# In the first of four batches, v of two heads as one stationary side; wide products of a pair's shared tile; the weights' clamp and rounding on other engines

## The chip, the cores and the metric

The kernel runs on one core of a Trainium2 chip, in one launch. The metric is device time in microseconds (us). Engines are named as in the profile: PE (TensorE matmul), PEld (its weight loads), DVE (VectorE), ACT (ScalarE), POOL (GpSimd), SP (the queue that issues most DMAs). All run side by side and wait for each other by semaphores; each takes its own instructions in program order.

## The reference

Three stages follow each other; everything is float32.

```
attention: B=4, H=8, S=576, D=64, blocks of 64, causal by block
  scores = q k^T / 8, masked where block(query) < block(key)
  attn = softmax(scores) (sum + 1e-9);  out = attn v;  x = out as (2304, 512)
first layer:  h = max(x w1, x w2, x w3);  x = h w_out        (512 -> 768 -> 512)
second layer: p = probs / sum(probs);  out = sum_e p_e * (relu(x w1_e) w2_e)   (4 experts, 512 -> 1024 -> 512)
```

## The kernel before

**Two halves for a float32 number.** A fast product type (F32R) keeps fewer bits than float32. Where precision matters, a number is split into a rounded high part and a low rest, and a product becomes three (high·high, high·low, low·high). The first batch of the attention works with plain float32 products instead, which PE carries out as two passes each: each such product shows as two MATMUL records, each with its own LDWEIGHTS.

**Attention.** Heads go in pairs (`NPAIR` is 4 pairs a batch, 16 in all). For a head, `scores` makes the transposed-sign score tiles (L250), takes row minima (DVE, L264), exponentials with row sums (ACT, L271), and leaves a `normalise` step (POOL, L282) for later. The last 64 queries of the two heads of a pair share one tile, `p4` (rows 0 to 63 are the even head's queries, 64 to 127 the odd one's). `turn_probs` transposes the probabilities on PE (L314) and evacuates them from PSUM into `eh` (batches 2 to 4: `eh` by ACT, L319, and the rest `el` by DVE, L320). Its part 2 is the shared tile: keys `j` = 0 to 4 by 128 columns, of which 64 belong to each head.

**The products with v.** `values` is the step that the change rewrites. In the first batch (`values32`, L341 and L345) the stationary side is one head's v block, 128 keys by 64 columns, so PE stands in a 128*64 arrangement; the fifth key block has 64 keys and gives 64*64. A head makes a 128-column product, then 384, 384, 128 and 256 columns, then five of 64 columns for its last 64 queries. All other products of the attention use 128 stationary columns. In batches 2 to 4 (L366, L374) the stationary side is `vs`, 128 columns: 64 of v's high part, 64 of its low part. `eh` and `el` are multiplied one after the other, and the last 64 queries take 5 products of 64 columns with `eh` and 5 with `el`. ACT copies half of the result (L385) and DVE adds the two halves (L386) into `xf`.

**The first layer.** `moe1(b)` runs as a filler between the steps of the next batch's attention, so many units per step (`UNITS`); in the last batch it runs by itself. Its products are L510, its running maximum L548 (DVE).

**The weights of the first layer** are computed once, in `Convert`: 26 pieces (18 of 512 columns for w1, w2, w3, 8 of 384 for w_out), beside the attention of batches 1 and 2. The inputs are 64-bit numbers, taken apart as words: per piece ACT makes `a` (L433) and `r` (L435); DVE clamps (L440), shifts (L442) and joins the sign (L443); POOL adds `r` (L447) and rounds to the high part (L82); DVE makes the low part (L457); a DMA stores both to `held`, from where batches 2 to 4 take them.

**What sets the order.** The code is recorded and a scheduler with a timeline of its own puts each engine's instructions in order, so an edit can move instructions that it does not touch. Buffers count too: the slots of `wt` (5), `r` (1), `a` (2) and `ps_x` (4 banks of PSUM) are reused when their last reader is done.

Of the kernel before, what the change touches and what calls it, by code (L numbers as in the profile page):

```python
# [25 lines left out]
def program(tc, q, k, v, w1, w2, w3, w_out, probs, e_w1, e_w2, out):  # L26
# [57 lines left out]
    def load_pair(g):  # L84
        b, h0 = divmod(2 * g, H)

        w = 2 * R * D
        o = (B - 1) * KD * S + g % 2 * w
        raw = arena[:, o:o + w].rearrange("p (r d) -> p r d", d=D)
        for n, src in ((0, q), (1, k)):  # L90
            for h, pp in ((0, lo), (1, hi)):
                nc.sync.dma_start(
                    out=raw[pp, n * R:(n + 1) * R],
                    in_=src[b, h0 + h].rearrange("(r p) d -> p r d", r=R),
                )
        vraw = ap_.tile([P, 2, 5, D], F32, name="vraw", tag="vraw", bufs=4)
        for h in range(2):
            nc.sync.dma_start(
                out=vraw[:, h, 0:4],
                in_=v[b, h0 + h, 0:512].rearrange("(j p) d -> p j d", p=P),  # L100
            )
        nc.sync.dma_start(
            out=vraw[hi, :, 4], in_=v[b, h0:h0 + 2, 512:S].rearrange("h p d -> p h d")
        )
        pairs[g] = dict(raw=raw, vraw=vraw)
# [19 lines left out]
    def prep_pair(g):  # L125
# [38 lines left out]
        for pp, js in ((both, slice(0, 4)), (hi, slice(4, 5))):  # L164
            vh = vs[pp, :, js, 0:64]
            rounded(nc.gpsimd, vh, vraw[pp, :, js])
            nc.gpsimd.tensor_tensor(vs[pp, :, js, 64:128], vraw[pp, :, js], f(vh), op=ALU.subtract)
# [131 lines left out]
    def turn_probs(g, part):  # L299
# [3 lines left out]
        w = (1024, 256, 640)[part]  # L303
        eh = ap_.tile([P, w], F32 if g < H else F32R, name="eh", tag=f"eh{part}", bufs=1)
        el = None if g < H else ap_.tile([P, w], F32R, name="el", tag=f"el{part}", bufs=1)
        (pairs[g // 2] if part == 2 else hd)["e", part] = (eh, el)
        pt = hd["p"] + [pairs[g // 2]["p4"]]
        for n in banks:
            o = 512 * (n - banks[0])
            tt = ps_x.tile([P, 512], F32, name="tt", tag="x")  # L310
            c = 0
            for j, i in BANKS[n]:
                k0 = S - P if j == 4 else j * P
                nc.tensor.transpose(tt[:, c:c + P], pt[i][:, k0:k0 + P], ident)  # L314
                c += P
            if g < H:
                (nc.scalar.copy if n else nc.vector.tensor_copy)(eh[:, o:o + c], tt[:, 0:c])
# [6 lines left out]
    def products(g, part):  # L324

        h = g % 2
        todo = []
        for j in KEYS[part]:
            q0 = max(P, P * j)
            todo.append((j, slice(q0 - P, 384), part, slice(BASE[j] + q0 - 512 * 2 * part, BASE[j] + 512 - 512 * 2 * part)))  # L330
        if part:
            todo += [(j, slice(384, 448), 2, slice(j * P + h * 64, j * P + h * 64 + 64)) for j in range(5)]
        return todo

    def values32(g, part):

        hd, vraw, h = heads[g], pairs[g // 2]["vraw"], g % 2
        if part == 0:
            hd["pv"] = [ps_v.tile([P, 512], F32, name=f"pv{i}", tag="v") for i in range(2)]
            et = hd["e", 0][0]  # L340
            nc.tensor.matmul(out=hd["pv"][0][lo, 0:P], lhsT=vraw[:, h, 0], rhs=et[:, 0:P], start=True, stop=True)  # L341
        for n, (j, to, which, of) in enumerate(products(g, part)):
            et = (pairs[g // 2] if which == 2 else hd)["e", which][0]
            rows = hi if j == 4 else both
            nc.tensor.matmul(  # L345
                out=hd["pv"][1][lo, to], lhsT=vraw[rows, h, j], rhs=et[rows, of],
                start=part == 0 and n == 0, stop=j == 4,
            )
# [3 lines left out]
        qs = (slice(0, P), slice(P, S))[part]  # L352
        nc.scalar.copy(xf[lo if h == 0 else hi, qs], hd["pv"][part][lo, 0:qs.stop - qs.start])
        if part:
            del heads[g]

    def values(g, part):
# [12 lines left out]
        todo = products(g, part)  # L370
        for n in range(2):
            for m, (j, to, which, of) in enumerate(todo):
                et = (pairs[g // 2] if which == 2 else hd)["e", which][n]
                nc.tensor.matmul(  # L374
                    out=pv[:, to], lhsT=vs[:, h, j], rhs=et[:, of],
                    start=part == 0 and n == 0 and m == 0, stop=part == 1 and n == 1 and j == 4,
                )
# [5 lines left out]
        src = hd["pv"][part][:, 0:qs.stop - qs.start]  # L383
        tmp = ap_.tile([P, S - P], F32, name="tmp", tag="tmp", bufs=1)[own, 0:qs.stop - qs.start]
        nc.scalar.copy(tmp, src[other])  # L385
        nc.vector.tensor_tensor(xf[own, qs], src[own], tmp, op=ALU.add)  # L386
        if part == 0:
            return
        del heads[g]
# [14 lines left out]
    class Convert:  # L404
# [32 lines left out]
        def second(self, i):  # L437
            a = self.buf(i, "a")
            au, high = a.bitcast(U32), self.words(i)[1]
            nc.vector.tensor_scalar(a, a, MOST, LEAST, op0=ALU.min, op1=ALU.max)  # L440
# [8 lines left out]
        def third(self, i):  # L449
# [6 lines left out]
            rounded(nc.gpsimd, high, a)  # L456
# [486 lines left out]
```

## Time and profile before

| | |
|---|---|
| median of 3 runs | 1324.93 us (1322.38 to 1325.15) |
| the profiled execution's time | 1325.09 us |
| its span | 1323.4 us |
| granted TensorE clock, mean | 0.991 |
| PE busy | 1286.8 us, 97% |
| PEld, DVE, POOL, ACT busy | 1185.8, 917.8, 629.9, 541.2 us |
| first to last product with v: batch 1 | 22.4 to 98.9 us |
| first to last product with v: batches 2 to 4 | 105.8 to 473.1 us |

A row of a group reads: line, engine, operation, tiles, shapes and count, then the busy time and the mean of one, then the idle time of the engine just before them and what ended it. A shape 128*64 is rows by columns of the stationary side; the one after it is partitions by moving columns. In a time line a row starts at the first number; how long a run of matmuls holds PE is read from its start to the start of the next row, because the ends overlap. Rows of waits give the total, the number and the longest.

### The profile page before, as it was taken

The page shows a single profiled execution, that of the slowest core. Times are in us where ns is not written, and L with a number is a line of the kernel's source. Part 1 is how long each engine was busy: PE and PEld are TensorE (multiplying, and loading weights), DVE is VectorE, ACT ScalarE, POOL GpSimd, SP SyncE. Part 2 cuts the span into 40 slices and gives each one's busy share as a digit, 9 for nine tenths or more (in the row PEclk, how much of TensorE's full clock was granted, in tenths as well). Part 3 has the DMA queues.
Part 4 walks back from the last instruction along what each step waited for, and adds up shares of the span by engine and source line. Part 5 has one row for each costly group of instructions (what it writes and reads, how often), then busy time and mean ns, then how long its engine had stood idle before and what let it go on. Part 6 is the DMA issues. An engine that isn't in the chain of part 4 may idle for free.

```text
span 1323.4 us, 20932 instructions
## 1 busy us (share of the span) xinstructions
PE 1286.8 (97%) x7670; PEld 1185.8 (90%) x7670; DVE 917.8 (69%) x1685; ACT 541.2 (41%) x1219; POOL 629.9 (48%) x639
## 2 busy tenths in 40 slices
PE   7899999999999999999999999999999999999998
PEld 5669889999999989988999998999999899999997
DVE  6878999555656562178767788777777876777753
ACT  5676666444544430143333343333333433333331
POOL 4965776333334342165444455444444644454420
PEclk9899999999999999999999999999999999999999
DMA  8746677555444355232222223222222133222211
GB/s 204 216 122 167 200 224 204 162 156 133 141 123 116 112 176 161 79 96 64 76 69 64 64 64 95 81 64 64 74 79 72 55 110 91 64 64 64 64 33 48
DMA packets 146982, 142.85 MB, mean 108 GB/s; under 512 B 64576, under 2 KB 112704, under 8 KB 146880
## 3 DMA queue, kind: packets, MB, share of 16 engines
q1 hardware_dynamic: 144480, 132.18, 34.0%
q10 hardware_dynamic: 2400, 9.34, 3.1%
q8 instruction: 60, 0.98, 0.3%
q14 instruction: 42, 0.34, 0.1%
HBM read 114.86 MB, written 17.30 MB: 100 GB/s over the span
## 4 chain that ended last, share of the span: by engine, by line
PE 79%; DVE 8%; issue 3%; DMA 3%; POOL 3%; ACT 2%; SPq 0%; ACTq 0%; POOLq 0%; DVEq 0%
PE m L796 24%; PE m L510 17%; PE o L861 10%; PE o L859 10%; PE o L860 10%; PE st L250 3%; PE pv L374 2%; PE tt L314 2%; DMA q<-q 1%; PE pv L345 1%; POOL p L282 1%; ACT p L271 1%; DVE arena L443 1%; DVE t L718 1%; DMA pr<-in_moe_domain_probs 1%
## 5 line engine op out<-in xcount | busy, mean ns | idle before, releaser
L510 PE MATMUL m<-xh,wt 128*128 128x288 f32 x1152 | 258.0, 302 | 6.5 <-DVE mt L548 5.5
L859 PE MATMUL o<-w2h,hh 128*128 128x512 f32 x576 | 225.4, 392 | 4.9 <-DVE arena L866 4.9
L861 PE MATMUL o<-w2h,hl 128*128 128x512 f32 x576 | 225.5, 392 | 1.3 <-DVE hl L824 1.3
L860 PE MATMUL o<-w2l,hh 128*128 128x512 f32 x576 | 225.2, 391 | 0.0
L510 PEld LDWEIGHTS m<-xh,wt 128*128 128x128 f32 x1152 | 191.4, 188 | 9.1 <-DVE mt L548 5.3
L824 DVE SCALAR_TENSOR_TENSOR hl<-c,hh 128x384 fp32r<-128x384 f32 x144 | 168.3, 1189 | 37.4 <-ACT hh L823 37.1
L689 POOL TENSOR_TENSOR w2l<-r,w2h 128x512 fp32r<-128x512 f32 x96 | 130.1, 1375 | 89.8 <-ACT w2h L688 89.8
L510 PE MATMUL m<-xl,wt 128*128 128x288 f32 x576 | 170.2, 295 | 0.0
L689 POOL TENSOR_TENSOR sl<-s,sh 128x1024 fp32r<-128x1024 f32 x48 | 116.6, 2429 | 77.5 <-ACT sh L688 77.5
L689 POOL TENSOR_TENSOR al<-r,ah 128x512 fp32r<-128x512 f32 x48 | 64.7, 1348 | 180.6 <-ACT ah L688 177.2
L866 DVE SCALAR_TENSOR_TENSOR arena<-o,pr,arena 128x512 f32<-128x512 f32 x126 | 93.6, 743 | 71.5 <-PE o L861 71.4
L859 PEld LDWEIGHTS o<-w2h,hh 128*128 128x128 f32 x576 | 108.6, 189 | 24.0 <-DVE arena L866 6.0
L861 PEld LDWEIGHTS o<-w2h,hl 128*128 128x128 f32 x576 | 108.5, 188 | 22.5 <-DVE hl L824 1.7
L823 ACT ACTIVATE hh<-c 128x384 fp32r<-128x384 f32 x144 | 71.0, 519 | 135.9 <-DVE c L818 135.9
L860 PEld LDWEIGHTS o<-w2l,hh 128*128 128x128 f32 x576 | 108.6, 189 | 17.8
L282 POOL TENSOR_SCALAR p<-p,sm 128x128 f32<-128x128 f32 (+2 forms) x144 | 89.4, 640 | 58.7 <-DVE sm L280 27.9
L510 PEld LDWEIGHTS m<-xl,wt 128*128 128x128 f32 x576 | 108.4, 188 | 0.7
L271 ACT ACTIVATE p<-st,mn 128x128 f32<-128x128 f32 (+3 forms) x144 | 78.7, 553 | 51.1 <-DVE mn L264 50.9
L688 ACT CAST ah<-r 128x512 fp32r<-128x512 f32 x48 | 29.8, 620 | 156.3 <-issue 124.2
L548 DVE TENSOR_TENSOR mt<-m,mt 128x288 f32<-128x288 f32 x96 | 43.5, 454 | 63.8 <-PE m L510 61.5
L510 PE MATMUL m<-hh,wo 128*128 128x288 f32 x384 | 84.5, 301 | 0.4 <-ACT arena L559 0.4
L688 ACT CAST w2h<-r 128x512 fp32r<-128x512 f32 x96 | 59.1, 619 | 44.3 <-PE o L861 35.0
(166 smaller groups left out, 3000.1 us busy)
## 6 DMA issues: line engine op xcount, KB each, us to landing
wt<-held SPq DMA_DIRECT2D x54, 512.0 KB, 4.0
r<-in_moe_w SPq DMA_DIRECT2D x48, 512.0 KB, 3.9
r<-in_moe_w SPq DMA_DIRECT2D x96, 256.0 KB, 2.7
arena<-in_moe_w SPq DMA_DIRECT2D x18, 512.0 KB, 4.5
held<-wt SPq DMA_DIRECT2D x18, 512.0 KB, 3.4
wo<-held SPq DMA_DIRECT2D x12, 768.0 KB, 4.3
q<-q ACTq DMA_DIRECT2D x26, 304.0 KB, 4.5
arena<-in_q SPq DMA_DIRECT2D x32, 144.0 KB, 3.3
```

What stands on the lines that cost most here:

```text
L271: nc.scalar.activation(x, st[:, o:o + w], ACTF.Exp, bias=mn[:, col:col + 1], scale=-1.0, accum_out=sm[:, col:col + 1],)
L282: nc.gpsimd.tensor_scalar(x, x, sm[:, col:col + 1], 1.0, op0=ALU.mult, op1=ALU.mult)
L510: nc.tensor.matmul(out=out_, lhsT=w, rhs=x, start=m == 0, stop=m == n - 1)
L688: nc.scalar.copy(dst_h, raw)
L689: (low or nc.gpsimd).tensor_tensor(dst_l, raw, f(dst_h), op=ALU.subtract)
L796: ins = nc.tensor.matmul(out=m, lhsT=w, rhs=x, start=start and n == 0, stop=stop and n == 3 * KH - 1, skip_group_check=True,)
L823: nc.scalar.activation(h, src, ACTF.Relu)
L824: nc.vector.scalar_tensor_tensor(l, src, 0.0, f(h), op0=ALU.max, op1=ALU.subtract)
L859: nc.tensor.matmul(out=o, lhsT=hh[:, ts], rhs=wh, start=i == 0, stop=False)
L860: nc.tensor.matmul(out=o, lhsT=hh[:, ts], rhs=wl, start=False, stop=False)
L861: nc.tensor.matmul(out=o, lhsT=hl[:, ts], rhs=wh, start=False, stop=i == G - 1)
L866: nc.vector.scalar_tensor_tensor(acc, ov, pr[:, tt, e:e + 1], acc, op0=ALU.mult, op1=ALU.add)
```

## The change

**First batch.** `vraw` is laid out key block by key block with the two heads side by side, so a stationary side is [128 keys, 128 columns] for both heads, and 64 result rows that belong to the other head are not used. Rows 0 to 63 of the fifth block are zeroed by POOL, and its product takes all 128 rows. The last 64 queries are left out of the even head and made once for the pair: five products of 128 columns (64 queries of each head) in the odd head. A head's rows are copied from where they lie, the odd head's with two more copies.

**Batches 2 to 4.** The shared tile is `e4`, with high and low part side by side. The five products of a head take 128 columns, high and low at once, instead of two times five of 64. The two results lie in columns 384 to 511: DVE adds the first half as before, and the second into `last`; in the odd head POOL adds `last` to `xf` for the pair.

**Weights.** The clamp goes from DVE to POOL, the rounding from POOL to ACT.

```diff
-        vraw = ap_.tile([P, 2, 5, D], F32, name="vraw", tag="vraw", bufs=4)
+        vraw = ap_.tile([P, 5, 2, D], F32, name="vraw", tag="vraw", bufs=4)
+        if g < NPAIR:
+            nc.gpsimd.memset(vraw[lo, 4], 0.0)
...
+        if part == 2:
+            e4 = ap_.tile([P, 5, 2, 2, 64], F32R, name="e4", tag="e4", bufs=1)
+            pairs[g // 2]["e4"] = e4
...
+            if part == 2:
+                j0, j1 = BANKS[n][0][0], BANKS[n][-1][0] + 1
+                high, low = (e4[:, j0:j1, :, x] for x in range(2))
+                src = tt[:, 0:c].rearrange("x (j h q) -> x j h q", h=2, q=64)
+                if g < H:
+                    nc.scalar.copy(f(high), src)
+                    continue
+                nc.scalar.copy(high, src)
+                nc.vector.tensor_tensor(low, src, f(high), op=ALU.subtract)
...
     def values32(g, part):
+        own = lo if h == 0 else hi
+        both_v = [vraw[:, j].rearrange("p h d -> p (h d)") for j in range(5)]
...
+        todo = [(j, to, et[:, of]) for j, to, of in products(part)]
+        if part and h:
+            todo += [(j, slice(384, 512), f(pairs[g // 2]["e4"][:, j, :, 0])) for j in range(5)]
+        for n, (j, to, x) in enumerate(todo):
             nc.tensor.matmul(
-                out=hd["pv"][1][lo, to], lhsT=vraw[rows, h, j], rhs=et[rows, of],
-                start=part == 0 and n == 0, stop=j == 4,
+                out=hd["pv"][1][:, to], lhsT=both_v[j], rhs=x,
+                start=part == 0 and n == 0, stop=part == 1 and n == len(todo) - 1,
             )
...
+        if h == 0:
+            nc.scalar.copy(xf[lo, P:512], pv[lo, 0:384])
+        else:
+            nc.scalar.copy(xf[hi, P:512], pv[hi, 0:384])
+            nc.scalar.copy(xf[lo, 512:S], pv[lo, 384:448])
+            nc.scalar.copy(xf[hi, 512:S], pv[hi, 448:512])
...
     def values(g, part):
+        todo = [(j, to, et[:, of]) for et in hd["e", part] for j, to, of in products(part)]
+        if part:
+            todo += [(j, slice(384, 512), pairs[g // 2]["e4"][:, j, h]) for j in range(5)]
+        for n, (j, to, x) in enumerate(todo):
+            nc.tensor.matmul(out=pv[:, to], lhsT=vs[:, h, j], rhs=x, start=part == 0 and n == 0, stop=j == 4)
...
+        last = pairs[g // 2]["last"]
+        nc.vector.tensor_tensor(last[own], src[own, w:n], tmp[:, w:n], op=ALU.add)
+        if h:
+            nc.gpsimd.tensor_tensor(xf[:, S - 64:S], xf[:, S - 64:S], last, op=ALU.add)
...
-            nc.vector.tensor_scalar(a, a, MOST, LEAST, op0=ALU.min, op1=ALU.max)
+            nc.gpsimd.tensor_scalar(a, a, MOST, LEAST, op0=ALU.min, op1=ALU.max)
...
-            rounded(nc.gpsimd, high, a)
+            rounded(nc.scalar, high, a)
```

The lines of the changed kernel are shifted: L341 and L345 become L359 and L368, L366 and L374 become L396 and L404, L385 and L386 become L414 and L415, L314 becomes L323, L176 L180, L250 L254; the clamp is L476 and the rounding L80.

**What stands in the queues.** PE, first batch, the end of an even head (`pv` is the result in PSUM, `tq` the transposes that prepare the next pair). Before:

```order
L345 MATMUL pv_612<-eh,vraw 64x256
L250 MATMUL st<-kk,q_376 128x256
L250 MATMUL st<-kk,q_377 128x256
L176 MATMUL tq<-idents,spare 128x128 x4
L345 MATMUL pv_612<-eh,vraw 64x64 x4
L176 MATMUL tq<-idents,spare 128x128 x8
L345 MATMUL pv_612<-eh,vraw 64x64
L176 MATMUL tq<-idents,spare 128x128 x6
```

Now:

```order
L368 MATMUL pv_613<-eh,vraw 128x256
L254 MATMUL st<-kk,q_380 128x256
L254 MATMUL st<-kk,q_381 128x256
L180 MATMUL tq<-idents,spare 128x128 x18
L323 MATMUL tt<-ident,p_489 128x128
```

The five narrow products are gone from the even head, and no row of 64 partitions is left between rows of 128. In the program before, the first batch's products with v stand in 32 such groups between other work.

PE, batch 2, its first head (`vs` is the split v). Before:

```order
L374 MATMUL pv_1206<-el,vs 128x128
L374 MATMUL pv_1206<-eh,vs 128x256
L374 MATMUL pv_1206<-eh,vs 128x64 x4
L250 MATMUL st<-kk,q_1096 128x128
L374 MATMUL pv_1206<-eh,vs 128x64
L374 MATMUL pv_1206<-el,vs 128x256
L374 MATMUL pv_1206<-el,vs 128x64 x5
```

Now:

```order
L404 MATMUL pv_1197<-el,vs 128x128
L404 MATMUL pv_1197<-eh,vs 128x256
L404 MATMUL pv_1197<-el,vs 128x256
L404 MATMUL pv_1197<-e_1184,vs 128x128 x4
L254 MATMUL st<-kk,q_1086 128x128
L404 MATMUL pv_1197<-e_1184,vs 128x128
```

Ten products of 64 columns became five of 128.

ACT, batch 2, the end of its second head (`arena` holds the conversion's `a` and `r`, `eh` the evacuated probabilities, `tmp` the copied half of a result). Before:

```order
L385 COPY tmp<-pv_1487 64x448
L319 CAST eh<-tt 128x512 x2
L319 CAST eh<-tt 128x256
L435 ACTIVATE arena<-arena 128x512
L319 CAST eh<-tt 128x512
L319 CAST eh<-tt 128x128
L385 COPY tmp<-pv_1659 64x128
```

Now:

```order
L414 COPY tmp<-pv_1475 64x512
L338 CAST eh<-tt 128x512 x2
L471 ACTIVATE arena<-arena 128x512
L80 CAST wt<-arena 128x512
L338 CAST eh<-tt 128x256
L469 ACTIVATE arena<-arena 128x512
L332 CAST e_1599<-tt 128x8x64
L332 CAST e_1599<-tt 128x2x64
L414 COPY tmp<-pv_1643 64x128
```

The rounding (L80) stands right behind `r` of the next piece (L471), ahead of evacuations. The last 4,387 products on PE, those from about 475 us of the span on, stand in the same order as before.

More of the change, by code (lines that the diff above doesn't have):

```diff
@@ L102, in load_pair @@
         nc.sync.dma_start(
-            out=vraw[hi, :, 4], in_=v[b, h0:h0 + 2, 512:S].rearrange("h p d -> p h d")
+            out=vraw[hi, 4], in_=v[b, h0:h0 + 2, 512:S].rearrange("h p d -> p h d")
         )
@@ L302, in turn_probs @@
         banks = PARTS[part]
[L303 to L306, printed above, removed]
+        if part == 2:
+            e4 = ap_.tile([P, 5, 2, 2, 64], F32R, name="e4", tag="e4", bufs=1)
+            pairs[g // 2]["e4"] = e4
+        else:
+            w = (1024, 256)[part]
+            eh = ap_.tile([P, w], F32 if g < H else F32R, name="eh", tag=f"eh{part}", bufs=1)
+            el = None if g < H else ap_.tile([P, w], F32R, name="el", tag=f"el{part}", bufs=1)
+            hd["e", part] = (eh, el)
         pt = hd["p"] + [pairs[g // 2]["p4"]]
@@ L322, in turn_probs, with products @@
             turn_probs(g, 2)
-    def products(g, part):
-        h = g % 2
+    def products(part):
         todo = []
@@ L337, in values32 @@
         hd, vraw, h = heads[g], pairs[g // 2]["vraw"], g % 2
+        own = lo if h == 0 else hi
+        both_v = [vraw[:, j].rearrange("p h d -> p (h d)") for j in range(5)]
         if part == 0:
             hd["pv"] = [ps_v.tile([P, 512], F32, name=f"pv{i}", tag="v") for i in range(2)]
[L340 to L345, printed above, removed]
-                out=hd["pv"][1][lo, to], lhsT=vraw[rows, h, j], rhs=et[rows, of],
-                start=part == 0 and n == 0, stop=j == 4,
+            nc.tensor.matmul(
+                out=hd["pv"][0][:, 0:P], lhsT=both_v[0], rhs=hd["e", 0][0][:, 0:P], start=True, stop=True
+            )
+        et = hd["e", part][0]
+        todo = [(j, to, et[:, of]) for j, to, of in products(part)]
+        if part and h:
+            todo += [(j, slice(384, 512), f(pairs[g // 2]["e4"][:, j, :, 0])) for j in range(5)]
+        for n, (j, to, x) in enumerate(todo):
+            nc.tensor.matmul(
+                out=hd["pv"][1][:, to], lhsT=both_v[j], rhs=x,
+                start=part == 0 and n == 0, stop=part == 1 and n == len(todo) - 1,
             )
@@ L351, in values32 @@
         xf = pairs[g // 2]["xf"]
[L352 to L355, printed above, removed]
+        if part == 0:
+            nc.scalar.copy(xf[own, 0:P], hd["pv"][0][own, 0:P])
+            return
+        pv = hd["pv"][1]
+        if h == 0:
+            nc.scalar.copy(xf[lo, P:512], pv[lo, 0:384])
+        else:
+            nc.scalar.copy(xf[hi, P:512], pv[hi, 0:384])
+            nc.scalar.copy(xf[lo, 512:S], pv[lo, 384:448])
+            nc.scalar.copy(xf[hi, 512:S], pv[hi, 448:512])
+        del heads[g]
     def values(g, part):
@@ L369, in values @@
         pv = hd["pv"][1]
[L370 to L377, printed above, removed]
+        todo = [(j, to, et[:, of]) for et in hd["e", part] for j, to, of in products(part)]
[3 more added lines that the diff above has]
+            nc.tensor.matmul(out=pv[:, to], lhsT=vs[:, h, j], rhs=x, start=part == 0 and n == 0, stop=j == 4)
         if part == 0 and h == 0:
@@ L382, in values @@
         qs = (slice(0, P), slice(P, S))[part]
-        src = hd["pv"][part][:, 0:qs.stop - qs.start]
-        tmp = ap_.tile([P, S - P], F32, name="tmp", tag="tmp", bufs=1)[own, 0:qs.stop - qs.start]
+        w = qs.stop - qs.start
+        n = (P, 512)[part]
+        src = hd["pv"][part][:, 0:n]
+        tmp = ap_.tile([P, 512], F32, name="tmp", tag="tmp", bufs=1)[own, 0:n]
         nc.scalar.copy(tmp, src[other])
-        nc.vector.tensor_tensor(xf[own, qs], src[own], tmp, op=ALU.add)
+        nc.vector.tensor_tensor(xf[own, qs], src[own, 0:w], tmp[:, 0:w], op=ALU.add)
         if part == 0:
             return
+        if h == 0:
+            pairs[g // 2]["last"] = ap_.tile([P, 64], F32, name="last", tag="last", bufs=1)
+        last = pairs[g // 2]["last"]
+        nc.vector.tensor_tensor(last[own], src[own, w:n], tmp[:, w:n], op=ALU.add)
+        if h:
+            nc.gpsimd.tensor_tensor(xf[:, S - 64:S], xf[:, S - 64:S], last, op=ALU.add)
         del heads[g]
```

12 lines of the change are left out of this document (6 added, 6 removed).

## The prediction

> **What bounds the kernel now.** I read the page's busy times and its chain first, then the busy times of all engines by stage.
>
> ```profile
> PE 1286.8 (97%) x7670; PEld 1185.8 (90%) x7670; DVE 917.8 (69%) x1685; ACT 541.2 (41%) x1219; POOL 629.9 (48%) x639
> PE 79%; DVE 8%; issue 3%; DMA 3%; POOL 3%; ACT 2%; SPq 0%; ACTq 0%; POOLq 0%; DVEq 0%
> ...
> core 0: us, PE busy (x) PEld busy (x) DVE busy (x) ACT busy (x) POOL busy (x), PEclk, DMA share, GB/s
> 0.00:50.00 50.00, 38.31 (x205) 30.17 (x205) 32.92 (x84) 27.33 (x72) 29.93 (x47) 0.93 0.82 201
> 50.00:100.00 50.00, 47.63 (x292) 33.84 (x290) 38.76 (x100) 36.24 (x104) 36.67 (x49) 0.93 0.59 161
> ...
> 100.00:230.00 130.00, 124.78 (x933) 120.20 (x932) 121.28 (x294) 81.50 (x208) 90.54 (x123) 1.00 0.68 200
> 230.00:355.00 125.00, 123.70 (x949) 122.36 (x950) 77.22 (x218) 62.25 (x173) 48.20 (x85) 1.00 0.54 148
> 355.00:475.00 120.00, 120.00 (x926) 119.45 (x926) 64.28 (x172) 51.69 (x140) 36.89 (x65) 1.00 0.41 121
> 475.00:1323.40 848.40, 832.36 (x4375) 759.81 (x4373) 583.29 (x821) 282.15 (x526) 387.67 (x273) 0.99 0.26 78
> ```
>
> The stretches are, in order, the start and first batch (0 to 100), batch 2 with the weights' conversion (100 to 230), batches 3 and 4 (to 475), and what the change leaves alone. In batches 3 and 4 PE is full and nobody else is near it: a microsecond of PE is a microsecond of the kernel. In 50 to 100 PE is busy 47.6 of 50, but its loads only 33.8: it waits for something inside itself. In 100 to 230 PE (124.8 of 130) and DVE (121.3) are both nearly full, so there both count. In 0 to 50 PE has 11.7 us of idle time.
>
> **Part 1: tails of batches 2 to 4.** The five pairs of 64-column products of a head.
>
> ```profile
> L374 PE MATMUL pv<-eh,vs 128*128 128x64 f32 x120 | 16.1, 256 | 0.0
> L374 PE MATMUL pv<-el,vs 128*128 128x64 f32 x120 | 15.7, 259 | 0.0
> ...
> 298.49 0.75 PE L374 MATMUL pv<-eh,vs 128*128 128x256 f32 x6
> 299.07 0.84 PE L374 MATMUL pv<-el,vs 128*128 128x256 f32 x6
> 299.75 0.38 PE L510 MATMUL m<-xh,wt 128*128 128x288 f32 x1
> ...
> 301.41 1.20 PE L250 MATMUL st<-kk,q 128*128 128x128 f32 x6
> ...
> 321.88 1.04 PE L314 MATMUL tt<-ident,p 128*128 128x128 f32 x8
> 322.68 0.38 PE L510 MATMUL m<-xh,wt 128*128 128x288 f32 x1
> ```
>
> Two products of 256 columns and ten of 64 hold PE from 298.49 to 299.75, 1.26 us. Twelve products of 288 columns then take 1.66 us, 0.138 each; with 0.13 for each of the two at 256, the ten cost 1.00, so 0.10 each. Eight matmuls of 128 columns (the transposes) take 0.80, also 0.10 each: at these widths the price is per product, not per column. So ten at 0.10 become five at 0.10: 0.50 us a head. The bounds: a 128-column product costs no more than a 288-column one (0.138), which leaves 1.00 - 0.69 = 0.31; and no less than 0.08 (were only the narrow side to count), which gives 0.60. Counts: 240 records become 120. Batches 3 and 4 have 16 heads: **8.0 us**, all on the path (5.0 to 9.6). Batch 2 has 8: 4.0 us of PE, counted in part 3.
>
> The Trainium skill, "TensorE: Matmul & The Clock Gate", section "LDWEIGHTS (loading the stationary operand)", prices a load by its columns, P/1.2 ns. That would be 107 ns for 128 columns, and by it the saving is 0.53 us a head, 8.5 in place of 8.0. The 0.10 of the rows agrees.
>
> **Part 2: the first batch.** Here PE goes back and forth between 64-wide and 128-wide stationary sides.
>
> ```profile
> 79.96 1.08 PE L345 MATMUL pv<-eh,vraw 128*64 128x384 f32 x4
> 80.97 0.33 PE L314 MATMUL tt<-ident,p 128*128 128x128 f32 x1
> 81.22 1.36 PE L345 MATMUL pv<-eh,vraw 128*64 128x256 f32 x12
> ...
> 88.28 0.65 PE L345 MATMUL pv<-eh,vraw 128*64 128x256 f32 x2
> 88.85 0.73 PE L250 MATMUL st<-kk,q 128*128 128x512 f32 x2
> ...
> L345 PEld LDWEIGHTS pv<-eh,vraw 128*64 128x64 f32 x128 | 12.1, 138 | 7.5 <-issue 5.0 <-ACT p L271 0.4 <-ACT arena L435 0.4
> L250 PEld LDWEIGHTS st<-kk,q 128*128 128x128 f32 x48 | 7.5, 204 | 3.1 <-ACT p L271 1.0 <-PE pv L341 0.8 <-DVE eh L317 0.6
> ```
>
> One transposition between two groups of 64-wide products takes 0.25 us (80.97 to 81.22) instead of 0.10: 0.15 for going out and coming back, on its side. On the other side: a group with two passes of 384 and two of 128 columns (1024 in all) takes 1.01 us, a group with two of 256 (512) takes 0.57; the slope is 0.86 ns a column, and 0.57 - 512 x 0.86 = 0.13 is left. A group thus costs 0.28 us beside its work. Its row of loads shows the same: 7.5 us idle, 5.0 of them on nothing that the profile names. The program has 32 groups, all gone: 32 x 0.28 = 9.0 us of PE time, some 24 of them (6.7 us) after 50 us.
>
> The last 64 queries: 20 passes of 64 columns a pair become 10 of 128.
>
> ```profile
> 52.06 0.68 PE L345 MATMUL pv<-eh,vraw 128*64 128x64 f32 x8
> 52.66 1.12 PE L176 MATMUL tq<-idents,spare 128*128 128x128 f32 x8
> ```
>
> Eight passes take 0.60 with their 0.13, so 0.06 each, 1.2 a pair; ten of 128 at 0.86 ns a column take 1.1. Nothing either way. The other 80 passes of the batch keep their columns. Their stationary side doubles to 128 columns; the rows have 138 ns for a load of 64 and 204 for one of 128, but a pass of 384 columns streams for 330, and loads overlap with it. Where no load were hidden, 80 x 0.066 = 5.3 us would be lost; I take nothing, since the load is shorter than the pass that covers it except at 128 columns.
>
> The Trainium skill, "TensorEngine Tiling (Array Packing)", section "Tiling Modes", states that changing the tiling mode drains the engine. No price is given there; the 0.28 us a group agrees with it.
>
> How much of 9.0 comes out: after 50 us PE is the bound, but DVE is at 38.8 of 50, so if PE gets 6.7 us shorter, DVE is at nine tenths and will be waited for here and there. I take 5.0 of the 6.7, and 0.5 of the 2.3 before 50 us, which lie beside 11.7 us of idle time: **5.5 us** (2 to 9). The additions are small: two copies of 64 columns in each odd head on ACT (36 of 50 busy), four memsets at the start.
>
> **Part 3: batch 2 and the conversion.**
>
> ```profile
> L440 DVE TENSOR_SCALAR arena<-arena 128x512 f32<-128x512 f32 x11 | 5.6, 510 | 0.8 <-ACT arena L433 0.7
> L386 DVE TENSOR_TENSOR xf<-pv,tmp 64x448 f32<-64x448 f32 x8 | 4.9, 616 | 0.1
> L440 DVE TENSOR_SCALAR arena<-arena 128x384 f32<-128x384 f32 x8 | 2.9, 368 | 0.5 <-ACT arena L433 0.4
> L386 DVE TENSOR_TENSOR xf<-pv,tmp 64x128 f32<-64x128 f32 x8 | 2.3, 285 | 0.1
> ...
> L82 POOL TENSOR_SCALAR wt<-arena 128x512 fp32r<-128x512 f32 x18 | 12.0, 668 | 8.5 <-PE m L510 7.8
> L167 POOL TENSOR_TENSOR vs<-vraw,vs 64x128 fp32r<-64x128 f32 x6 | 3.7, 623 | 0.5
> ...
> L688 ACT CAST ah<-r 128x512 fp32r<-128x512 f32 x48 | 29.8, 620 | 156.3 <-issue 124.2
> ...
> PE m L510 <- DVE mt L548: 3.5, 4, 1.4
> ...
> POOL arena L447 <- DVE arena L443: 10.9, 7, 3.8
> ...
> ACT arena L435 <- POOL arena L447: 15.3, 10, 3.2
> ```
>
> DVE loses 19 clamps in this stretch, 5.6 + 2.9 = 8.5 us. It gains eight additions into `last` of 64 columns: from 285 ns at 128 columns and 616 at 448 the slope is 1.03 ns, so 0.22 each, 1.8 us. Net 6.7 of its 121.3. The evacuation of `e4` has the same elements as that of `eh` and `el` before. POOL gives up the rounding and takes the clamp, both a TENSOR_SCALAR of the same size: I take the same 0.67, and at most 0.62 for each pair's addition of `last`, 2.5 in 90.5 of 130. ACT gains 19 roundings of some 0.6 (row of 512 columns: 620 ns), 11 us on 81.5 of 130, and 64 columns more on each `tmp`: it has room.
>
> The step's place matters more than its length. Clamp and rounding now cross engines twice more per piece. Behind the clamp in POOL's queue stand `normalise` (PE's transposes wait for it) and hh/hl; behind the rounding in ACT's queue stand exponentials and evacuations. But the rounding waits for POOL's addition, and ACT waited for that same addition before, for the single `r` buffer: 15.3 us in 10 waits. The rounding stands right behind that wait in the new order, so it adds its length and not a second wait. What POOL waited for weight slots (7.8 us) goes over to ACT; it lies at the start of batch 2, before PE uses up the first slots.
>
> So PE needs 4.0 us less and DVE 6.7 less, where both are nearly full, and PE's waits for DVE's running maximum (3.5 us) should shrink. Alone, PE's part would give two thirds (2.7), DVE's rather more: I take **5.0 us** (1 to 9; below by the hand-overs, above by all of DVE's and the waits).
>
> **The sum.** 8.0 + 5.5 + 5.0 = 18.5 us off the profiled execution's 1325.1 us (its span 1323.4 and 1.7 around it): 1306.6. That execution lies 0.2 us above the median of the runs shown, 1324.9, so the forecast is **1307 us**. Ends: 5 + 2 + 1 = 8 gives 1317, 9.6 + 9 + 9 = 27.6 gives 1297.
>
> **The rivals.**
>
> First batch bound elsewhere (0.14). If DVE, POOL and the transfers set its pace, or if the wider loads show, part 2 gives nothing: 1306.6 + 5.5 = 1312, and with exposed loads up to 1317. For it: PE idle in 0 to 50, DVE at 38.8. Against: PE at 47.6 of 50. By the Trainium skill's section on loading the stationary operand ("TensorE: Matmul & The Clock Gate"), 53 ns more on each of 80 passes would be 4.3 us, an estimate worked out from that page. No row here has a float32 pass with 128 stationary columns beside one with 64.
>
> Everything comes out (0.15). All of the 6.7 us after 50 us with some of those before, 9 in batch 2: 1297.
>
> Width counts in batches 2 to 4 (0.06). If 128 columns cost twice 64, parts 1 and the 4.0 us of PE are gone, and 5.5 + 2 remain: 1318. Against it stand the 0.10 us of both widths.
>
> Slower (0.05): the rounding blocks ACT. Should each of the 26 pieces hold ACT for a further 1.5 us (15.3 over 10, the mean of its wait on POOL's addition) and PE wait for the evacuations behind it, 39 us would be lost against 18.5 gained: 1345. It decides from 18.5/26 = 0.71 us a piece. Against it: ACT is idle 48 of 130 us, and the order puts the rounding behind a wait that is there anyway.
>
> **How the numbers follow.** The forecast has 0.60, with its own range 1300 to 1314; the rivals 0.14, 0.15, 0.06, 0.05. The range of 8 in 10 is 1297 to 1317. This kernel's measurement cannot tell less than about 0.2% (2.6 us) from no change. The forecast, the first two rivals and nearly all of the third are faster; the fourth is slower, and small versions of it and of the third make the middle: faster 0.92, same 0.03, slower 0.05.
>
> **What would show it.** Part 1: 120 products of 128 columns in place of 240, ten becoming five in a block that shrinks from 1.26 to about 0.75 us; batches 3 and 4 still full on PE and 8 us shorter together. Part 2: no 128*64 row; a single transposition between products with v at 0.10 us, not 0.25; the last product of batch 1 some 5 us before 98.9. Part 3: DVE's busy time in batch 2 about 7 us lower, waits of PE for L548's successor smaller. Wrong would be a new wait of PE on ACT's evacuations, or ACT's rounding waiting on PE for weight slots with exponentials behind it, or a batch 1 that ends at the same time with DVE or POOL named as releaser.

## The result and the profile after

The changed kernel takes 1303.88 us (median of 4 runs, 1299.98 to 1305.38), the kernel before beside it 1324.48; the ratio is 0.9836, with a 95% interval of 0.982 to 0.9853. The forecast was 1307 with 1297 to 1317. The profiled execution took 1305.38 us, its span 1303.5.

The page's line of busy times and the stretches that the prediction used, of the kernel after (columns as before):

```profile
PE 1263.9 (97%) x7510; PEld 1176.6 (90%) x7510; DVE 902.9 (69%) x1683; ACT 554.7 (43%) x1253; POOL 634.4 (49%) x655
...
0.00:50.00 50.00, 37.41 (x220) 32.54 (x221) 36.21 (x93) 34.16 (x95) 34.24 (x56) 1.00 0.87 218
50.00:100.00 50.00, 45.63 (x294) 40.39 (x292) 37.73 (x93) 37.38 (x107) 34.22 (x46) 0.93 0.61 157
100.00:230.00 130.00, 125.59 (x928) 122.67 (x928) 119.22 (x310) 96.18 (x246) 93.65 (x132) 0.97 0.69 204
```

PE lost 22.9 us of busy time, ACT gained 13.5. The stretches compare less well than they look, since the products with v of batch 2 stand 7 to 18 us earlier in them. So the rest of this document cuts each trace where the work changes: at the start of the last product of the first batch with v, and at the first product of the second layer. Of before, then of after:

```profile
0.00:98.90 98.90, 84.84 (x485) 62.97 (x486) 71.68 (x183) 63.17 (x174) 65.50 (x94) 0.93 0.70 180
98.90:562.50 463.60, 453.80 (x3443) 446.49 (x3443) 293.98 (x727) 212.57 (x554) 205.50 (x304) 1.00 0.53 154
```

```profile
0.00:90.30 90.30, 74.16 (x442) 64.28 (x443) 69.03 (x175) 65.92 (x185) 67.22 (x100) 0.96 0.77 197
90.30:544.50 454.20, 442.94 (x3327) 437.33 (x3326) 282.04 (x733) 223.33 (x577) 208.13 (x315) 0.99 0.55 157
```

Three numbers come out of such a row: its length, PE's idle time (length less busy time), and PE's busy time times the granted clock, which is about what the work would take at full clock. (Only about, since the row's clock is a mean over idle time too. Taking from the busy time half of what lies in the stretches at half clock comes closer; the table further down does so.) In the first stretch PE's work went from 84.84 x 0.93 = 78.9 to 74.16 x 0.96 = 71.2 us (by the stretches at half clock, 79.2 and 70.8), its idle time from 14.1 to 16.1, and the stretch became 8.6 us shorter. The second became 9.4 us shorter: 10.9 less busy, 1.5 more idle. Together 18.0; the second layer, which the change does not touch, differs by 1.9 (760.9 and 759.0 us).

The edits themselves did to PE what was worked out. In the time line of the kernel after, one transposition between products with v (72.42) and the tails of the first batch and of batch 3 (281.57):

```profile
72.42 0.27 PE L323 MATMUL tt<-ident,p 128*128 128x128 f32 x1
72.53 0.60 PE L368 MATMUL pv<-eh,vraw 128*128 128x256 f32 x2
72.96 1.28 PE L368 MATMUL pv<-e,vraw 128*128 128x128 f32 x10
74.08 0.93 PE L323 MATMUL tt<-ident,p 128*128 128x128 f32 x7
...
281.57 0.28 PE L404 MATMUL pv<-eh,vs 128*128 128x256 f32 x1
281.69 0.28 PE L404 MATMUL pv<-el,vs 128*128 128x256 f32 x1
281.81 0.67 PE L404 MATMUL pv<-e,vs 128*128 128x128 f32 x5
282.31 0.28 PE L254 MATMUL st<-kk,q 128*128 128x128 f32 x1
```

The transposition holds PE for 0.11 us (before 0.25). Ten passes of 128 columns take 1.12 (forecast 1.1). The block of two products of 256 columns and the tails takes 0.74 (before 1.26, forecast 0.75). What is new are waits. Of the kernel after, waits of PE, ACT and POOL between 100 and 230 us (total, times, longest):

```profile
POOL arena L476 <- ACT arena L469: 14.7, 8, 9.1
...
PE m L546 <- DVE wo L493: 1.9, 1, 1.9
...
ACT arena L471 <- POOL arena L483: 1.2, 2, 0.9
```

POOL's clamp waits for ACT's first step; PE has no wait for POOL in that stretch. PE waits once for the low part of w_out weights, and the clock is halved during that wait (from 200.4 us on). ACT's wait for POOL's addition, 15.3 us before, is all but gone.

### The profile page after: what moved, and what is told of

Its sections match the earlier page's. It is cut to its first block, busy times and chain, and to the rows that moved or that the text cites. A ratio compares the mean times of both kernels' runs of the same rounds, so it can differ in the third digit from the quotient of the medians.

```text
span 1303.5 us, 20657 instructions
## 1 busy us (share of the span) xinstructions
PE 1263.9 (97%) x7510; PEld 1176.6 (90%) x7510; DVE 902.9 (69%) x1683; ACT 554.7 (43%) x1253; POOL 634.4 (49%) x655
## 4 chain that ended last, share of the span: by engine, by line
PE 82%; DVE 8%; DMA 4%; issue 2%; ACT 2%; POOL 2%; ACTq 0%; SPq 0%; DVEq 0%; POOLq 0%
PE m L832 24%; PE m L546 19%; PE o L897 10%; PE o L896 10%; PE o L895 10%; PE st L254 4%; PE pv L404 2%; DMA q<-q 2%; PE tt L323 2%; DVE mn L268 1%; DMA wo<-held 1%; ACT p L275 1%; DVE hl L860 1%; DVE t L754 1%; PE tq L199 1%
## 5 line engine op out<-in xcount | busy, mean ns | idle before, releaser
L546 PE MATMUL m<-xh,wt 128*128 128x288 f32 x1152 | 254.6, 301 | 2.8 <-DVE mt L584 2.0
L859 ACT ACTIVATE hh<-c 128x384 fp32r<-128x384 f32 x144 | 71.1, 519 | 135.2 <-DVE c L854 135.2
L286 POOL TENSOR_SCALAR p<-p,sm 128x128 f32<-128x128 f32 (+2 forms) x144 | 86.5, 618 | 48.5 <-DVE sm L284 26.0
L275 ACT ACTIVATE p<-st,mn 128x128 f32<-128x128 f32 (+3 forms) x144 | 78.9, 556 | 35.7 <-DVE mn L268 35.2
L254 PE MATMUL st<-kk,q 128*128 128x256 f32 (+4 forms) x336 | 75.1, 338 | 6.0 <-DMA q<-q 4.9
```

The costliest lines, as they stand in the source:

```text
L254: nc.tensor.matmul(out=st[:, o + c:o + c + n], lhsT=pair[part][:, q0:q0 + P], rhs=pair["kk"][:, x, c:c + n], start=m == 0, stop=m == len(t ...
L275: nc.scalar.activation(x, st[:, o:o + w], ACTF.Exp, bias=mn[:, col:col + 1], scale=-1.0, accum_out=sm[:, col:col + 1],)
L286: nc.gpsimd.tensor_scalar(x, x, sm[:, col:col + 1], 1.0, op0=ALU.mult, op1=ALU.mult)
L546: nc.tensor.matmul(out=out_, lhsT=w, rhs=x, start=m == 0, stop=m == n - 1)
L859: nc.scalar.activation(h, src, ACTF.Relu)
```

## The experiments

The three parts, each alone, and the two with products together. The medians of these four stand against 1324.9 us of before (17 runs).

**The first batch's part alone:** `vraw` in the new layout, both heads as stationary side, one tail for the pair; batches 2 to 4 and the weights as before.

```diff
...
-                out=hd["pv"][1][lo, to], lhsT=vraw[rows, h, j], rhs=et[rows, of],
+                out=hd["pv"][1][:, to], lhsT=both_v[j], rhs=x,
...
```

> The first batch's part alone: 128 stationary columns, the tail once per pair; batches 2 to 4 and the weights as before. Theory (PE is the bound of the first batch, the groups' switching is its loss): 5.5 to 8.5 us faster than before, about 1317, the last product of batch 1 at 90 to 93 us. Rival (part of the 8.7 us that the whole change gained up to there came from DVE, which lost its clamps, or from a clock that happened to be full): 2 to 4 us, about 1321, and waits of PE for DVE in batch 1.

Measured: 1329.41 us, ratio 1.003 (1.0019 to 1.0041). Neither expectation held: this part by itself costs 4.5 us. Its two stretches:

```profile
0.00:98.60 98.60, 79.98 (x446) 68.99 (x447) 71.16 (x183) 63.56 (x180) 66.15 (x99) 0.90 0.71 182
98.60:564.60 466.00, 454.06 (x3444) 448.08 (x3443) 293.68 (x727) 213.72 (x556) 203.86 (x303) 1.00 0.53 153
```

PE's work in batch 1, by the stretches at half clock, is 70.6 us, 8.6 less than before. But its idle time grew by 4.5 (18.6), the half clock cost 9.4 us in place of 5.7 (the mean clock fell from 0.93 to 0.90), and the batch ended when it had ended before. The waits of PE from 20 to 100 us name the place; above this kernel, below before:

```profile
PE tq L179 <- ACT p L274: 5.8, 4, 2.8
PE tt L317 <- ACT p L274: 1.8, 2, 1.0
```

```profile
PE tq L176 <- ACT p L271: 1.8, 1, 1.8
```

How one of them comes about shows in the time line of POOL, ACT and PE (idle time and releaser in brackets), and in the stretches around it:

```profile
65.70 3.63 POOL L285 TENSOR_SCALAR p<-p,sm 128x128 f32<-128x128 f32 x3
69.30 1.26 POOL L464 TENSOR_TENSOR arena<-arena 128x512 int32<-128x512 int32 x1
...
70.59 0.67 ACT L452 ACTIVATE arena<-arena 128x512 int32<-128x512 uint32 x1 [1.72 <-POOL arena L464]
71.16 0.35 ACT L274 ACTIVATE p<-st,mn 128x128 f32<-128x128 f32 x1
71.50 0.57 ACT L274 ACTIVATE p<-st,mn 128x384 f32<-128x384 f32 x1
72.06 0.68 ACT L274 ACTIVATE p<-st,mn 128x512 f32<-128x512 f32 x1
...
72.22 2.00 PE L179 MATMUL tq<-idents,parts 128*128 128x128 f32 x9 [2.79 <-ACT p L274]
...
69.20:72.60 3.40, 0.61 (x5) 0.41 (x5) 3.38 (x9) 2.01 (x6) 1.36 (x2) 1.00 0.69 211
72.60:79.40 6.80, 6.80 (x32) 6.64 (x32) 3.25 (x11) 5.23 (x17) 5.31 (x8) 0.50 0.62 169
```

POOL normalises until 69.3 and only then makes a weight piece's addition. ACT's next step in the queue needs that addition, for the single `r` buffer, and waits 1.72 us with three exponentials behind it. PE's transpositions need a PSUM bank that the first two of these exponentials read, and wait 2.79. So PE was busy 0.61 of 3.40 us, and then had 6.8 us at half clock, which cost a further 3.4.

The faster products are not all that differs here. The edit does not touch ACT's step, but the scheduler placed it anew. Counted from the start of the program it is the step of the seventh piece, and the exponentials behind it are the 28th to 30th. Of the kernel before, the 28th exponential, the one of 512 columns (the 31st there) and the step of the seventh piece:

```profile
69.10 0.37 ACT L271 ACTIVATE p<-st,mn 128x128 f32<-128x128 f32 x1 [0.47 <-DVE mn L264]
...
72.10 0.68 ACT L271 ACTIVATE p<-st,mn 128x512 f32<-128x512 f32 x1
...
73.64 0.66 ACT L435 ACTIVATE arena<-arena 128x512 int32<-128x512 uint32 x1
```

Before, the step stood behind the exponentials and waited for nothing; here it stands ahead of them. The run of both products and the one without a clamp, further down, have it ahead as well, and their batch 1 ends latest (102.1 and 102.2). The run of the rounding alone has it ahead too and ends batch 1 at 96.6. No run held the order fixed, so how much of the loss is the faster products' and how much the new order's stays open.

**Batches 2 to 4 alone** (the first batch keeps its 64-wide products and reads its last queries from the new tile):

```diff
...
-    w = (1024, 256, 640)[part]
+    e4 = ap_.tile([P, 5, 2, 2, 64], F32R, name="e4", tag="e4", bufs=1)
...
+        todo += [(j, slice(384, 512), pairs[g // 2]["e4"][:, j, h]) for j in range(5)]
...
```

> The wide products of batches 2 to 4 alone; the first batch's products 64 wide as before (they read the new tile), weights as before. Theory (0.10 us a product whatever its width): 120 fewer products, 12 us of PE, of which 10 to 11 come out: 1313 to 1315. Rival (in batch 2 DVE is as full as PE and hides its third): 8 us, 1316.5. Rival (width counts): 3 us or less.

Measured: 1312.94 us, ratio 0.9905 (0.9892 to 0.9917): 12.0 us, a little more than the theory expected. The second stretch:

```profile
96.80:551.60 454.80, 442.31 (x3323) 434.89 (x3324) 295.49 (x751) 214.73 (x554) 213.32 (x316) 1.00 0.54 157
```

PE's busy time there is 11.5 us below before's 453.80. By the prediction's 0.50 us a head, 24 heads give 12.0. But of the 12.3 us by which this trace is shorter, the stretch has only 8.8, since its idle time rose from 9.8 to 12.5. Batch 2, from its first product of 384 columns to that of batch 3, before and here:

```profile
105.80:234.00 128.20, 122.74 (x915) 117.93 (x915) 121.62 (x294) 80.70 (x207) 91.60 (x124) 1.00 0.67 201
103.60:231.90 128.30, 120.01 (x884) 114.79 (x883) 122.18 (x302) 83.27 (x208) 97.23 (x128) 1.00 0.69 204
```

Batch 2 takes as long as before: PE's shorter work became idle time there (5.5 to 8.3 us), as the rival had it; that DVE is what holds it is not shown. From there to the second layer it is 328.5 us before and 319.7 here, 8.8 less (forecast 8.0 for batches 3 and 4). Four products of the first layer, some 0.6 us, moved across that cut, which takes a little from the 8.8 and gives it to batch 2. The rest, 2.1 us of batch 1 and 1.4 of the second layer, lies where PE's products are the old ones. What made it was not tried; that the sum came to 12 is in part luck.

**The weights' part alone:**

```diff
-            nc.vector.tensor_scalar(a, a, MOST, LEAST, op0=ALU.min, op1=ALU.max)
+            nc.gpsimd.tensor_scalar(a, a, MOST, LEAST, op0=ALU.min, op1=ALU.max)
...
-            rounded(nc.gpsimd, high, a)
+            rounded(nc.scalar, high, a)
```

> The clamp on POOL and the rounding on ACT alone, all products as before. Theory (DVE relieved by 6.7 us net in batch 2): 2 to 5 us faster, 1320 to 1322. Rival (two more crossings a piece make the last pieces late, as the wait of 1.9 us for the last weights in the changed kernel hints): no change or up to 3 us slower, 1324 to 1328.

Measured: 1311.56 us, ratio 0.99 (0.9887 to 0.9913): 13.3 us. Both expectations were far off. Its two stretches:

```profile
0.00:93.50 93.50, 82.66 (x485) 60.71 (x486) 67.53 (x176) 64.79 (x179) 66.52 (x97) 0.96 0.74 191
93.50:553.00 459.50, 453.43 (x3442) 449.18 (x3443) 285.17 (x708) 223.10 (x575) 201.94 (x300) 0.99 0.54 155
```

PE's idle time fell from 14.1 to 10.8 and from 9.8 to 6.1 us, with the same products. Batch 1 ended 5.4 us earlier: the conversion reaches into it (7 of its 26 pieces), which the forecast left out.

**Both products, without the weights' part:**

```diff
-            nc.gpsimd.tensor_scalar(a, a, MOST, LEAST, op0=ALU.min, op1=ALU.max)
+            nc.vector.tensor_scalar(a, a, MOST, LEAST, op0=ALU.min, op1=ALU.max)
...
-            rounded(nc.scalar, high, a)
+            rounded(nc.gpsimd, high, a)
```

(against the kernel after)

> The whole change without the weights' part: both sets of products new, clamp on DVE and rounding on POOL as before. Theory (parts add up): 2 to 5 us slower than the whole change's 1304, so 1306 to 1309. Rival (the weights' part gives nothing, or costs): 1304 or less.

Measured: 1314.52 us, ratio 0.9914 (0.9901 to 0.9927). Neither expectation came out; this is 10 us behind the whole change. With the wide products the first batch's part gives nothing again (1312.94 without it; the intervals overlap). Batch 1 ended at 102.1, and the wait of the same transpositions is 8.1 us between 20 and 103:

```profile
PE tq L180 <- ACT p L275: 8.1, 4, 4.1
```

The next four runs were made together, against 1324.98 us of before (29 runs). **The whole change without its first part:** the run of batches 2 to 4 alone, with the edit of the weights' part.

> The change without its first part: batch 1 has its 64-wide products, batches 2 to 4 the wide ones, the weights' clamp and rounding lie on POOL and ACT. Theory (the first batch's part is worth nothing of its own, because exponentials that come late hold PE there): the two gains add, 1324.9 - 12.0 - 13.3 = 1300, at most 2 off, so as fast as the whole change (1304) or faster. Rival (once the weights' work is off DVE, a shorter PE does shorten batch 1, by the forecast's 5.5): 1309 to 1310, slower than the whole change. Batch 1 ends at 93 to 94 by the theory as in the run of the weights' part alone; the whole change has 90.3.

Measured: 1305.77 us, ratio 0.986 (0.9847 to 0.9873), beside 0.9836 (0.982 to 0.9853) of the whole change. This lies between the two expectations, and it cannot be told apart from the whole change. By the medians the first batch's part is worth 1.9 us here.

```profile
0.00:93.10 93.10, 82.44 (x485) 60.91 (x486) 66.74 (x176) 65.23 (x179) 66.91 (x97) 0.96 0.74 192
```

Set against the kernel after: PE's work in batch 1 falls by 8.4 us (79.2 to 70.8) with that part, its idle time rises by 5.4 (10.7 to 16.1), and the batch ends 2.8 earlier. The trace gives that back: from the end of batch 1 to the second layer it is 450.4 us here and 454.2 in the kernel after.

**The two moves of the weights' part, one by one.** The clamp only:

```diff
-            nc.vector.tensor_scalar(a, a, MOST, LEAST, op0=ALU.min, op1=ALU.max)
+            nc.gpsimd.tensor_scalar(a, a, MOST, LEAST, op0=ALU.min, op1=ALU.max)
```

> The kernel before with the clamp on POOL, the rounding still on POOL. Theory (the gain of the weights' part is DVE's relief: 26 clamps of 0.37 to 0.51 us, 12.1 us in all, before row minima and running maxima that others wait for): most of the 13.3, 1314 to 1317. Rival (it is the shorter hand-over of a piece: ACT no longer waits 15.3 us for POOL's addition): nothing, or slower by the longer queue on POOL, 1325 to 1330.

Measured: 1321.29 us, ratio 0.9974 (0.9964 to 0.9983). The rounding only:

```diff
-            rounded(nc.gpsimd, high, a)
+            rounded(nc.scalar, high, a)
```

> The kernel before with the rounding on ACT, the clamp still on DVE. Theory (DVE's relief is the gain): DVE has as much to do as before, so little comes, 1320 to 1325. Rival (POOL's queue is the cause: 18 roundings of 0.67 us and 8 shorter ones leave it, so that additions and normalisations come earlier): most of the 13.3, 1313 to 1317.

Measured: 1323.82 us, ratio 0.9997 (0.9986 to 1.0007). And no clamp at all:

```diff
-            nc.vector.tensor_scalar(a, a, MOST, LEAST, op0=ALU.min, op1=ALU.max)
```

> The kernel before with the clamp left out altogether (so the computation lacks that step); DVE loses 12.1 us and no other engine gains any. Theory (DVE's relief is the gain): at least as much as the clamp's move gives, 1312 to 1316. Rival (the piece's way through the engines, or POOL's load): 1322 to 1325.

Measured: 1323.87 us, ratio 0.9992 (0.9983 to 1.0001). So 3.7 and 1.2 us for the moves alone, 13.3 for both, and DVE's relief without a move 1.1 (1.2 and 1.1 cannot be told from nothing). The clamp's run misses both of its expectations; the rounding's lies where DVE's relief as the cause would have it, the one without a clamp where its rival would have it. No theory of a single cause stands: neither lighter DVE nor lighter POOL is enough. Nor is it enough that ACT's wait for POOL's addition goes (15.3 us before, between 100 and 230 us). With the clamp's move alone it is nearly gone, at a gain of 3.7:

```profile
ACT arena L435 <- POOL arena L447: 2.5, 2, 2.0
```

What each move alone left shows in PE's waits over the whole program. First the clamp's move, then the rounding's, then both:

```profile
PE st L250 <- DMA q<-q: 5.2, 6, 2.0
PE m L510 <- DVE mt L548: 2.0, 1, 2.0
```

```profile
PE st L250 <- DMA q<-q: 4.4, 6, 1.2
PE m L510 <- DVE mt L548: 2.6, 2, 2.0
```

```profile
PE m L510 <- DVE mt L548: 2.0, 1, 2.0
PE st L250 <- DMA q<-q: 1.1, 2, 0.6
```

Each alone shrinks the wait for the running maximum (5.5 us before) and puts one for a transfer of `q` in its place, which ACT issues (1.1 before). The whole change has 4.9 us of that wait as well, so it does not tell these two from it. Why the transfer comes late was not tried. Each of these kernels also has its own order of instructions, and no run separates a move from the order that came with it. Without the clamp, batch 1 even ended 3.3 us later, at 102.2, with the clock at 0.90:

```profile
0.00:102.20 102.20, 89.07 (x486) 66.16 (x486) 66.73 (x176) 62.79 (x174) 63.35 (x94) 0.90 0.68 175
```

**With most of the conversion's arithmetic left out.** Clamp, shift, joining of the sign, low words and addition are gone, in the kernel before and in the one with the first batch's part alone (before 1325.44 us, 9 runs).

```diff
-            nc.scalar.activation(self.buf(i, "r").bitcast(I32), low, ACTF.Copy, scale=2.0 ** -29)
...
         def second(self, i):
...
-            nc.vector.tensor_scalar(a, a, MOST, LEAST, op0=ALU.min, op1=ALU.max)
...
+            return
```

> The kernel before with most of the weights' arithmetic left out (clamp, shift, joining of the sign, low words and their addition; the weights are therefore not the reference's): DVE loses three of four operations a piece, ACT and POOL one each. It is the base for the next run. If the conversion's load on DVE, ACT and POOL makes the waits of batches 1 and 2, PE's idle time before the second layer falls from 23.9 us to some 10 and the time to 1305 to 1312; if the waits are the attention's own chain, it stays above 1318.

Measured: 1310.56 us, ratio 0.9889 (0.9876 to 0.9903): the time of the first reading, though idle time fell less than it had it (17.0 us).

> The same, with the first batch's part of the change. Theory (the 9 us of PE time that come out are eaten because minima, exponentials and evacuations stand behind the conversion's operations): with these gone, this run is 5 to 9 us faster than the previous one. Rival (the first batch's own chain of scores, minima, exponentials and transpositions sets its pace, conversion or not): 2 us faster to 4 slower, as in the run of this part on the kernel before (4 slower), with PE's idle time in batch 1 longer by what its busy time is shorter.

Measured: 1307.04 us, ratio 0.9861 (0.9847 to 0.9874). First and second kernel:

```profile
0.00:94.70 94.70, 83.13 (x485) 61.04 (x486) 55.30 (x162) 58.19 (x166) 50.71 (x87) 0.96 0.75 188
94.70:549.50 454.80, 449.40 (x3442) 446.02 (x3443) 260.79 (x670) 203.44 (x536) 176.32 (x285) 1.00 0.55 157
```

```profile
0.00:88.00 88.00, 72.59 (x446) 62.38 (x446) 53.76 (x162) 59.15 (x172) 53.38 (x92) 0.98 0.81 204
88.00:543.40 455.40, 449.99 (x3444) 446.17 (x3443) 261.73 (x670) 204.41 (x538) 175.88 (x284) 1.00 0.54 157
```

With the other engines light, the first batch's part does shorten the kernel: 3.5 us by the medians, 6.1 by the two traces up to the second layer (the second kernel's profiled execution, 1304.62, lies below its median). The sign is the theory's, the median's size below it: 9.2 us of work go, 3.8 come back as idle time. The 8.0 us between this gain and the 4.5 us lost with the arithmetic in place come with that arithmetic, by its load or by the order of instructions that it brings. That the idle time still grows without it suggests that part of the chain is the attention's own; this was not tried. The other reading of these rows: taking nearly all arithmetic out brings PE's idle time to 17.0 us (11.6 + 5.4), which both moves together reach as well (10.8 + 6.1 = 16.9). By idle time, clamp and rounding moved together take away as much as leaving this arithmetic out does.

**Two attempts at a faster version of the whole change.** The conversion recorded one weight tile ahead:

```diff
-            self.upto(sum(i <= n for i, _ in pieces))
+            self.upto(sum(i <= n + 1 for i, _ in pieces))
```

> The whole change, with the conversion recorded one weight tile further ahead of its use. In the changed kernel PE waits 1.9 us at 201 us for the low part of a w_out piece, and the clock is halved from 200.4 to 207.2. Theory (the late piece causes both): both go, 1.9 + 3.4 = 5.3 us, 1298 to 1300. Rival (the piece is late since ACT, DVE and POOL are full there, wherever it is recorded): 1302 to 1306.

Measured: 1303.74 us, ratio 0.9829 (0.9815 to 0.9844), the same as the change. The late weights still held PE for 1.9 us; the rival's number came out. Three `a` and two `r` buffers, and two for the raw words:

```diff
-            o, each, bufs = dict(raw=(0, 1024, 3), a=(3072, 512, 2), r=(4096, 512, 1))[kind]
+            o, each, bufs = dict(raw=(0, 1024, 2), a=(2048, 512, 3), r=(3584, 512, 2))[kind]
```

> The whole change with the conversion's buffers in the same space shared out differently: three for a and two for r, in place of two and one, and two for the raw words in place of three. Theory (what is left of the waits in batches 1 and 2 is the conversion's buffers: ACT waits 7.4 us in 7 waits for a's last reader, and the w_out piece that stalls PE at 201 us comes late through that): PE's idle time before the second layer falls from 27.4 us by 4 to 6, the half-clock stretch at 200 us goes, 1296 to 1300. Rival (ACT, DVE and POOL are simply busy there, and two raw buffers make the loads late): 1302 to 1308.

Measured: 1312.52 us, ratio 0.9916 (0.9891 to 0.9941). This run settles nothing. With two raw buffers the load of the piece after next overwrites a piece's words before their sign is joined, so the weights here carry the sign of others, and DVE's joining waits for those loads (5.1 us up to 230 us). Whether a second `r` buffer alone would take the wait of ACT away stays open. No version faster than the change was found.

## Why the prediction was right, and where it was not

The total, 18.5 us off, was about right (20.6 by the medians, 19.7 by the profiled executions), but two of its three terms were wrong and made up for each other, which is luck. The times of the runs, in us against the kernel before beside them, and for batch 1 PE's work at full clock, what the stretches at half clock cost (half of PE's busy time in them; in the kernel before they are 31.0 to 37.9 and 54.9 to 61.8), and its idle time. The three add up to the batch's end:

| kernel | time | batch 1 ends | PE work | half clock | PE idle |
|---|---|---|---|---|---|
| before | | 98.9 | 79.2 | 5.7 | 14.1 |
| first batch's part | +4.5 | 98.6 | 70.6 | 9.4 | 18.6 |
| batches 2 to 4 | -12.0 | 96.8 | 79.7 | 5.1 | 12.0 |
| weights' part | -13.3 | 93.5 | 79.6 | 3.1 | 10.8 |
| both products | -10.4 | 102.1 | 71.1 | 9.6 | 21.4 |
| batches 2 to 4 and weights | -19.2 | 93.1 | 79.2 | 3.2 | 10.7 |
| the whole change | -20.6 | 90.3 | 70.8 | 3.4 | 16.1 |
| little arithmetic | -14.9 | 94.7 | 80.1 | 3.0 | 11.6 |
| the same, first batch's part | -18.4 | 88.0 | 70.9 | 1.7 | 15.4 |

**Part 1 was right**, in price and place: the block went from 1.26 to 0.74 us (0.50 a head forecast), and the run of the wide products alone is 8.8 us shorter from batch 3 to the second layer (8.0). The 4.0 us of batch 2, counted in part 3, did not come out in that run: its 12.0 have 3.5 us from elsewhere in their place. The rival that width counts is out: five products of 128 columns took 0.50 us. The bound of 0.08 for one of them stands on no row.

**Part 2: the work was right, what comes out of it was not.** "32 x 0.28 = 9.0 us of PE time" is borne out by four pairs of runs: 8.6, 8.6, 8.4 and 9.2 us less work. The loads of 128 columns cost nothing that shows. The step that failed is "after 50 us PE is the bound ... I take 5.0 of the 6.7". PE was busy 47.6 of 50 there, but at a granted clock of 0.93, so that some 3 us of this were the halved clock and not work. And the saved work did not come out: in all four pairs idle time grew by 3.8 to 9.4 us, and in two of them the half clock cost 3.7 and 4.5 us more. Where it was followed, PE waited for ACT's exponentials, which waited behind a conversion step for POOL's addition, in an order that the scheduler had made anew. Whether the chain would be as long in the old order is not shown. Measured: 4.5 us lost alone, nothing with the wide products, 1.9 us on top of the other two (not told apart from nothing), 3.5 with the arithmetic gone. The first rival (batch 1 bound elsewhere, "part 2 gives nothing") described this; it named DVE, POOL and transfers, and the place that was followed is ACT behind POOL. That batch 1 ended 8.6 us earlier in the whole change, as if part 2 had done it, is mostly the weights' part: 5.4 of it come without the products.

**Part 3 was mis-sized**: "I take 5.0 us (1 to 9)" for PE's 4.0 and DVE's 6.7 together. Of the 5.0, 2.7 were PE's part, which belongs to the wide products. That leaves 2.3 for the weights, which brought 13.3 alone, 10.2 on top of both products, and 7.2 on top of batches 2 to 4 (by the table). Two steps failed. It was priced by the length of the operations moved in batch 2, though batch 1 holds 7 of the 26 pieces and gained 5.4 us. And of the wait of ACT for POOL's addition, 15.3 us, the text said "it adds its length and not a second wait": it took the wait as given. In the whole change this wait is 1.2 us. But with the clamp's move alone it is 2.5 us at a gain of 3.7, so its going is not by itself what brought the time. The waits for the running maximum shrank as said. Why it takes both moves is not settled; the moves' own effect and the order of instructions that came with them stand side by side as causes.

DVE's busy time in 100 to 230 us fell by 2.1, not 7. The window holds other work now, since batch 2 stands earlier in it; over the program it fell by 14.9. The slower rival (rounding blocks ACT) did not come: POOL waits for ACT's first step instead, and PE not for ACT's evacuations.

## What to carry to other kernels

Cut a trace where the work changes and write each piece as PE's work at full clock, plus what the halved clock cost, plus idle time: a saving of work that does not come out then shows at once, as idle time or half clock that grows. Cut it again before a median is called as expected: the wide products' 12 us came in part from other places than the 12 that were forecast. An operation moved to another engine is not priced by its own length, and here not by the wait that it removes either: taking away most of 15 us of an engine's waiting gave 3.7 us. Two parts that give little alone can give much together (3.7 and 1.2 us, and 13.3), so they are to be run in both ways before either is called useless. And where a scheduler orders the instructions, compare the order of the queues too: an edit can put a waiting step ahead of work that it stood behind.

## What the hardware showed that was not expected

PE can fall to half clock after a stretch in which it was only partly idle, and such idle time then costs more than its own length. In the first batch's part alone it was busy 0.61 of 3.40 us and then had 6.8 us at 0.50 (rows above). Of the kernel after, around PE's wait for the w_out weights, and a stretch later on with what follows it:

```profile
196.80:200.40 3.60, 2.26 (x12) 1.22 (x10) 3.57 (x14) 3.58 (x10) 3.06 (x6) 1.00 0.35 119
200.40:207.20 6.80, 5.69 (x24) 5.67 (x25) 5.06 (x14) 4.18 (x12) 4.64 (x8) 0.50 0.36 123
...
241.40:244.80 3.40, 1.88 (x16) 1.67 (x15) 1.58 (x4) 1.02 (x3) 0.00 (x0) 1.00 0.91 196
244.80:248.20 3.40, 3.40 (x28) 3.40 (x26) 0.69 (x2) 0.00 (x0) 1.25 (x2) 1.00 0.59 168
```

In the first, PE was busy 2.26 of 3.60 us, and 6.8 us at half clock followed, a loss of some 2.8 us (half of the 5.69 busy). In the second it was busy 1.88 of 3.40, a smaller share, and kept its full clock. So the busy share of such a stretch does not decide by itself; what does, these traces do not show. The Trainium skill, "TensorE: Matmul & The Clock Gate", section "Part 1: The HAM clock gate (the "warmup" mystery)", has the clock halved after at least one idle window of about 3.4 us. The lengths agree, 6.8 being two of them; but neither of the two stretches ahead of a half clock was idle throughout, and here the measurement decides.
